# Weight casts moved from VectorE to ScalarE, and a third buffer for w_out, in a talking-heads attention and MLP kernel

## The chip, the cores and the metric

The kernel runs on one core of a Trainium2 chip. The metric is device time in microseconds (us) of one execution. The engines are TensorE (PE: matmul; PEld: its weight load), VectorE (DVE), ScalarE (ACT), GpSimd (POOL) and SyncE (SP, which here only issues DMAs).

## The reference, cut to what matters

Attention over 4 batches, 12 heads, 448 positions, head size 64, with a mix of the heads before and after the softmax; then an MLP over the 1792 tokens that come out of it:

```python
x = attn_out.transpose(0, 2, 1, 3).reshape(1792, 768)
h = x @ w_in                    # w_in  768 x 2048, float64
g = np.maximum(0.01 * h, h)
out = (g @ w_out).astype(np.float32)   # w_out 2048 x 768, float64
```

The two MLP weights come as float64 and have to become float32 on the chip.

## The kernel before, in words

**Stages.** The attention runs in 16 chunks of up to 120 query rows (4 per batch). While it runs, most of the weights are narrowed: float64 pieces of 128x384 are loaded, turned to float32 (`Narrow`, L78 to L111) and stored in a scratch tensor `w_dram`. For w_in, and for the first two blocks of w_out, this happens there. The other 14 blocks of w_out (`EARLY <= i < NF`, L321) are narrowed in the MLP itself, in its first pass.

**The MLP** has 4 passes (one for each batch, 448 tokens), each over NF = 16 blocks of 128 hidden features, so 64 blocks i. `hidden(i)` (L341) multiplies the block of w_in (part 0) with x: 18 matmuls into `psh`; ScalarE scales the result (t, L350), VectorE takes the maximum (g, L351), ScalarE casts it to float32r (gh, L352), and VectorE takes the rest (gl, L353). `project(i)` (L356) multiplies the block of w_out (part 1) with g: 18 matmuls into `pso`. Eighteen, because each float32 operand is split into a float32r value and a rest, and three of the products are made for each of 6 slices (`three`, L336).

**A weight block** comes to SBUF by `load_w(i, part)` (L319). Its tile is `wr`; part 0, and part 1 of blocks 0, 1 and from 16 on, is one DMA from `w_dram` (L325). Part 1 of blocks 2 to 15 is narrowed into `wr` in two pieces: DMA of the float64 words (craw, L90), two ScalarE copies (z, L100, and w or wr, L101), three VectorE operations (top L102, top L105, exp L108), two GpSimd operations (L109, L110), and a DMA that saves the float32 piece for later passes (L111). `prep_w(i, part)` (L328) splits the block: `wh` is the cast to float32r (L332, VectorE), `wl` the rest (L333, VectorE). All weight tags (wr, wh, wl of each part) have two buffers, from pool `w`.

**Order.** The loop at L489 writes, for i = 1 to 64: prep_w(i, 1), prep_w(i+1, 0), hidden(i), load_w(i+2, 0), load_w(i+1, 1), project(i-1), and at a pass's end the loads and splits of the next x. Dependencies and waits are put in by the framework, which also orders each engine's instructions at compile time from this program order and its own estimate of when each is ready. On the chip every engine takes its instructions in that fixed order. In the trace VectorE's order in a block of the first pass differs from the program's. Blocks 0 and 1 are loaded and block 0 and part 0 of block 1 split during the last attention chunk (L465 to L475).

The few lines that matter most:

```python
t = pl["w"].tile([P, DM], F32, tag=f"r{part}", name=f"wr{part}")   # L320
nc.vector.tensor_copy(hi, raw)                                      # L332
nc.vector.tensor_sub(lo, raw, hi.bitcast(F32))                      # L333
if i + 1 < n:                                                       # L499
    load_w(i + 1, 1)
```

Of the kernel before, what the change touches and what calls it, by code (L numbers as in the profile page):

```python
# [8 lines left out]
F32 = mybir.dt.float32  # L9
# [23 lines left out]
def kernel(  # L33
# [10 lines left out]
    nc = tc.nc  # L44
    B, P, NJ, H, D = v.shape
    S = k.shape[3]
    DM = out.shape[0]
# [248 lines left out]
    pl = {}  # L296
# [10 lines left out]
    def load_x(b, c):  # L307
        xr_t[b, c] = pl["xr"].tile([P, S], F32, tag="xr", name="xr")
        nc.sync.dma_start(xr_t[b, c], x_dram[b][:, c])

    def prep_x(b, c):
        raw = xr_t.pop((b, c))
        hi = pl["xs"].tile([P, S], F32R, tag="xh", name="xh")
        lo = pl["xs"].tile([P, S], F32R, tag="xl", name="xl")
        nc.scalar.copy(hi, raw)
        nc.vector.tensor_sub(lo, raw, hi.bitcast(F32))
        x_t[b, c] = hi, lo

    def load_w(i, part):  # L319
        t = pl["w"].tile([P, DM], F32, tag=f"r{part}", name=f"wr{part}")  # L320
        if part and EARLY <= i < NF:  # L321
            for j in range(2):
                Narrow(pl["n"], i, 2 + j, t[:, j * PIECE:(j + 1) * PIECE])()
        else:
            nc.sync.dma_start(t, w_dram[i % NF][:, part * DM:(part + 1) * DM])  # L325
        wr_t[i, part] = t

    def prep_w(i, part):  # L328
        raw = wr_t.pop((i, part))
        hi = pl["w"].tile([P, DM], F32R, tag=f"h{part}", name=f"wh{part}")  # L330
        lo = pl["w"].tile([P, DM], F32R, tag=f"l{part}", name=f"wl{part}")
        nc.vector.tensor_copy(hi, raw)  # L332
        nc.vector.tensor_sub(lo, raw, hi.bitcast(F32))  # L333
        w_t[i, part] = hi, lo

# [5 lines left out]
    def hidden(i):  # L341
        ps = pl["ps_h"].tile([P, 512], F32, tag="h", name="psh")
        for c in range(NC):
            three(ps[:, :S], w_t[i, 0], x_t[i // NF, c], c, c == 0, c == NC - 1)
        del w_t[i, 0]
        t = pl["g"].tile([P, S], F32, tag="t", name="t", bufs=1)
        g = pl["g"].tile([P, S], F32, tag="g", name="g", bufs=1)
        hi = pl["g"].tile([P, S], F32R, tag="gh", name="gh")
        lo = pl["g"].tile([P, S], F32R, tag="gl", name="gl")
        nc.scalar.activation(t, ps[:, :S], AF.Copy, scale=0.01)  # L350
        nc.vector.tensor_max(g, t, ps[:, :S])  # L351
        nc.scalar.copy(hi, g)  # L352
        nc.vector.tensor_sub(lo, g, hi.bitcast(F32))  # L353
        g_t[i] = hi, lo

    def project(i):  # L356
        b, f = divmod(i, NF)
        w, g = w_t.pop((i, 1)), g_t.pop(i)
        for c in range(NC):
            if f == 0:  # L360
                o_t[c] = pl["ps_o"].tile([P, 512], F32, tag=f"o{c}", name=f"pso{c}")
            three(o_t[c][:, :S], w, g, c, f == 0, f == NF - 1)
            if f == NF - 1:
                o = pl["o"].tile([P, S], F32, tag="o", name="o")
                (nc.scalar.copy, nc.vector.tensor_copy)[c % 2](o, o_t[c][:, :S])
                (nc.scalar, nc.sync)[c % 2].dma_start(out[c * P:(c + 1) * P, b * S:(b + 1) * S], o)
# [23 lines left out]
    for t, pat in ((kraw, ((H, ROWS), (0, H))), (kpost, ((0, H), (H, ROWS)))):  # L390

        nc.gpsimd.affine_select(
            t, t, pattern=[[-a, z] for a, z in pat], base=0, channel_multiplier=1, compare_op=ALU.is_ge, fill=0.0
        )
        nc.gpsimd.affine_select(
            t, t, pattern=[[a, z] for a, z in pat], base=H - 1, channel_multiplier=-1,
# [18 lines left out]
    for n in range(NCK):  # L415
# [4 lines left out]
        for t in range(SLOTS):  # L420
# [44 lines left out]
            if last and t == NC:  # L465
                load_w(0, 0)
                load_w(0, 1)
                load_w(1, 0)
            if last and t == NC + 2:
                prep_w(0, 0)  # L470
                prep_w(0, 1)
                load_w(1, 1)
            if last and t == NC + 4:
                prep_w(1, 0)
                load_w(2, 0)  # L475
# [10 lines left out]
    pl.update(o=pool("o", NC), n=pool("n", 2), ps_o=pool("ps_o", 1, space=PSUM))  # L486

    n = B * NF
    for i in range(1, n + 1):  # L489
        b, f = divmod(i, NF)  # L490
        if i < n:
            prep_w(i, 1)
        if i + 1 < n:
            prep_w(i + 1, 0)
        if i < n:
            hidden(i)
        if i + 2 < n:
            load_w(i + 2, 0)
        if i + 1 < n:  # L499
            load_w(i + 1, 1)  # L500
        project(i - 1)

        if b + 1 < B:
            for c in range(NC):
                if f == NF - 4 + (c > 3):
                    load_x(b + 1, c)
            if f == NF - 3:
                for c in range(4):
                    prep_x(b + 1, c)
            if f == NF - 1:  # L510
                for c in range(4, NC):
                    prep_x(b + 1, c)
# [39 lines left out]
```

## Time and profile before

| | us |
|---|---|
| median of 3 runs | 1094.42 |
| the 3 runs | 1094.42, 1084.62, 1095.0 |
| the profiled execution, device time | 1095.89 |
| its span, first to last instruction | 1094.2 |

The span is what the profile divides up; the 1.7 us between it and the device time lie around it. Busy time counts an instruction from start to end as the profiler records it, waits for a memory port included; matmuls overlap, so their durations add up to more than the time that they take. In rows of the timeline the first number is the start and the second the length in us; "x2" merges two instructions of one kind that follow each other, and a bracket gives the idle time before and what ended it.

### The profile page before, as it was taken

To read this page: it belongs to the slowest core of one execution; us is meant where nothing else is said; L and a number is where in the kernel's file an instruction comes from. 1 tells how busy PE (TensorE), PEld (TensorE's weight loads), DVE (VectorE), ACT (ScalarE), POOL (GpSimd) and SP (SyncE) were. 2 spreads that over 40 slices of the span, in tenths; PEclk is the share of its full clock that TensorE was granted. 3 is DMA by queue.
4 is the path that set the end of the run, shared out by engine and by line. 5 is a ranking of instruction groups with operands and counts; after the bars stand their busy time and mean duration, and the time that the engine had idled before them with its cause. 6 is when DMAs were issued, how large, how long until landed. Compare 5 with 4: busy or idle time off the path is not lost. (4 is left out here: it accounts for less than half of the span.)

```text
span 1094.2 us, 17821 instructions
## 1 busy us (share of the span) xinstructions
PE 1012.1 (93%) x6564; PEld 842.9 (77%) x6564; DVE 839.4 (77%) x1390; ACT 424.6 (39%) x951; POOL 444.6 (41%) x356
## 2 busy tenths in 40 slices
PE   4899889997899999999999988889999999999998
PEld 2576667775777767677768777779999999999997
DVE  6899887789888999768797599997556755565553
ACT  3664365644645646455552233332112211121111
POOL 5677764578565676546441165661000000000000
PEclk9999889998999999899999999999999999999999
DMA  5746533764354624536263455566333634353421
GB/s 184 282 161 194 190 110 119 234 198 156 119 171 158 240 70 154 177 112 216 100 230 89 136 181 177 178 179 214 102 116 103 205 102 116 104 163 101 116 89 63
DMA packets 93771, 167.11 MB, mean 153 GB/s; under 512 B 26740, under 2 KB 68724, under 8 KB 93172
## 3 DMA queue, kind: packets, MB, share of 16 engines
q1 hardware_dynamic: 91956, 163.23, 47.0%
q10 hardware_dynamic: 1728, 2.75, 0.7%
q8 instruction: 51, 0.84, 0.3%
q14 instruction: 36, 0.29, 0.1%
HBM read 103.82 MB, written 23.59 MB: 116 GB/s over the span
## 5 line engine op out<-in xcount | busy, mean ns | idle before, releaser
L211 POOL TENSOR_TENSOR rlo<-rt,rhi 120x448 fp32r<-120x448 f32 x144 | 175.3, 1221 | 141.6 <-DVE rhi L210 82.2
L332 DVE CAST wh<-wr 128x768 fp32r<-128x768 f32 x128 | 88.7, 695 | 138.3 <-PE psh L339 88.4
L256 PEld LDWEIGHTS psa<-kp,et 120*128 120x128 f32 (+2 forms) x1800 | 166.0, 174 | 35.7 <-issue 18.2
L256 PE MATMUL psa<-kp,et 120*128 120x120 f32 (+2 forms) x1800 | 179.8, 262 | 13.2 <-DVE kp L229 9.4
L216 ACT ACTIVATE et<-psm,stat 120x448 f32<-120x448 f32 x180 | 114.7, 639 | 152.7 <-DVE stat L215 151.3
L214 PE MATMUL psm<-rhi,kpre 120*120 120x448 f32 x360 | 149.5, 420 | 22.0 <-ACT et L216 21.7
L339 PE MATMUL pso<-gh,wl 128*128 128x448 f32 x384 | 141.7, 371 | 14.0 <-DVE wl L333 13.4
L339 PE MATMUL psh<-xh,wl 128*128 128x448 f32 x384 | 140.6, 366 | 3.5 <-DVE g L351 3.5
L339 PE MATMUL pso<-gl,wh 128*128 128x448 f32 x384 | 141.4, 368 | 0.0
L339 PE MATMUL pso<-gh,wh 128*128 128x448 f32 x384 | 141.4, 368 | 0.0
L339 PE MATMUL psh<-xh,wh 128*128 128x448 f32 x384 | 140.6, 366 | 0.0
L339 PE MATMUL psh<-xl,wh 128*128 128x448 f32 x384 | 140.4, 366 | 0.0
L350 ACT ACTIVATE t<-psh 128x448 f32<-128x448 f32 x64 | 34.8, 544 | 252.5 <-PE psh L339 243.2
L210 DVE CAST rhi<-rt 120x448 fp32r<-120x448 f32 x180 | 129.0, 717 | 2.3 <-DMA rt<-st 2.3
L215 DVE TENSOR_REDUCE stat<-psm 120x1 f32<-120x448 f32 x180 | 110.4, 614 | 26.4 <-PE psm L214 26.2
L333 DVE TENSOR_TENSOR wl<-wr,wh 128x768 fp32r<-128x768 f32 x128 | 123.8, 968 | 1.6
L187 ACT ACTIVATE st<-pss 120x448 f32<-120x448 f32 (+1 forms) x192 | 97.1, 551 | 57.4 <-PE pss L186 27.4
L282 PE MATMUL psx<-at,vt 128*64 128x120 f32 (+1 forms) x1152 | 109.0, 282 | 4.1 <-DVE at L264 2.7
L214 PEld LDWEIGHTS psm<-rhi,kpre 120*120 120x120 f32 x360 | 68.9, 191 | 47.0 <-ACT et L216 31.9
L282 PEld LDWEIGHTS psx<-at,vt 128*64 128x64 f32 x1152 | 68.0, 141 | 43.8 <-issue 31.5
L186 PE MATMUL pss<-kst,qlo 128*120 128x448 f32 (+1 forms) x192 | 82.3, 428 | 20.1 <-POOL kst L146 10.2
L339 PEld LDWEIGHTS pso<-gh,wl 128*128 128x128 f32 x384 | 72.9, 190 | 24.1 <-issue 14.5
(64 smaller groups left out, 1658.7 us busy)
## 6 DMA issues: line engine op xcount, KB each, us to landing
wr<-w_dram SPq DMA_DIRECT2D x114, 384.0 KB
rt<-st SPq DMA_DIRECT2D x176, 210.0 KB
craw<-in_w_moe SPq DMA_DIRECT2D x64, 384.0 KB
kraw<-in_k SPq DMA_DIRECT2D x48, 224.0 KB
qraw<-in_q SPq DMA_DIRECT2D x11, 720.0 KB
w_dram<-w SPq DMA_DIRECT2D x36, 192.0 KB
vt<-in_v SPq DMA_DIRECT2D x4, 1536.0 KB
xr<-x_dram SPq DMA_DIRECT2D x24, 224.0 KB
```

Of the source, the lines that this page charges most:

```text
L186: nc.tensor.matmul(ps[:m, :S], w[:, h, :m], k_t[b, h], start=i == 0, stop=i == 1)
L187: nc.scalar.activation(s_t[n][:m, h, :], ps[:m, :S], AF.Copy, scale=scale)
L210: nc.vector.tensor_copy(hi[:kk], raw[:kk])
L211: (nc.vector if g == 3 else nc.gpsimd).tensor_sub(lo[:kk], raw[:kk], hi[:kk].bitcast(F32))
L214: nc.tensor.matmul(ps[:kk, :S], kpre[w][:kk, :sg[g][1], :], x[:kk], start=i == 0, stop=i == 2)
L215: nc.vector.tensor_reduce(st[:kk, 0, g:g + 1], ps[:kk, :S], axis=AX.X, op=ALU.max, negate=True)
L216: nc.scalar.activation(e[:kk], ps[:kk, :S], AF.Exp, bias=st[:kk, 0, g:g + 1], accum_out=st[:kk, 1, g:g + 1])
L256: nc.tensor.matmul(ps[p0:p0 + np, w * g:w * g + nh * r], es[g][:r * H, c * P:c * P + np], kp[:r * H, g, h::step, :r], start=True, stop=True,)
L282: nc.tensor.matmul(ps[D * e:D * (e + 1), pair % 3, :m], v_t[b][up, c, h, :], at[:, c, h, :m] if c < NJ - 1 else half[up, pair, :m], start= ...
L332: nc.vector.tensor_copy(hi, raw)
L333: nc.vector.tensor_sub(lo, raw, hi.bitcast(F32))
L339: nc.tensor.matmul(ps, w[a][:, c * P:(c + 1) * P], x[e], start=first and j == 0, stop=last and j == 2)
```

## The change

`wh` is made by ScalarE's copy in place of VectorE's. Part 1 of a weight block (w_out) has three `wr` buffers in place of two and is loaded, and in blocks 2 to 15 narrowed, two blocks ahead in place of one; block 2 is loaded ahead of the loop. Part 0 keeps two buffers.

```diff
     def load_w(i, part):
-        t = pl["w"].tile([P, DM], F32, tag=f"r{part}", name=f"wr{part}")
+        t = pl["w"].tile([P, DM], F32, tag=f"r{part}", name=f"wr{part}", bufs=2 + part)
...
     def prep_w(i, part):
...
-        nc.vector.tensor_copy(hi, raw)
+        nc.scalar.copy(hi, raw)
         nc.vector.tensor_sub(lo, raw, hi.bitcast(F32))
...
     n = B * NF
+    load_w(2, 1)
     for i in range(1, n + 1):
...
         if i + 2 < n:
             load_w(i + 2, 0)
-        if i + 1 < n:
-            load_w(i + 1, 1)
+        if i + 2 < n:
+            load_w(i + 2, 1)
         project(i - 1)
```

## Rows read from the trace of the kernel before

**Rows 1.** The page: busy time by engine, and VectorE's busy tenths in 40 slices

```profile
PE 1012.1 (93%) x6564; PEld 842.9 (77%) x6564; DVE 839.4 (77%) x1390; ACT 424.6 (39%) x951; POOL 444.6 (41%) x356
...
DVE  6899887789888999768797599997556755565553
```

**Rows 2.** Windows: stretch, length, busy time by engine, TensorE's clock, DMA share, GB/s

```profile
560.00:577.00 17.00, 14.71 (x136) 10.36 (x134) 17.00 (x29) 8.87 (x22) 9.87 (x8) 0.90 0.69 225
...
616.78:745.00 128.22, 111.23 (x515) 98.16 (x516) 116.89 (x173) 45.10 (x92) 74.71 (x56) 0.97 0.60 181
...
750.00:1082.24 332.24, 332.24 (x1641) 307.87 (x1640) 192.68 (x285) 57.55 (x104) 0.00 (x0) 1.00 0.41 120
```

**Rows 3.** The chain that ended last, two pieces of the later passes

```profile
768.51 3.65 PE pso L339 x18
772.16 3.65 PE psh L339 x18
```

**Rows 4.** Waits, 592 to 745 us: total, times, longest

```profile
ACT wr L101 <- DVE wl L333: 40.0, 12, 4.8
...
PE pso L339 <- DVE wl L333: 13.4, 10, 2.7
```

**Rows 5.** Groups of instructions by line, 620 to 742 us

```profile
L109 POOL TENSOR_TENSOR wr<-wr,exp 128x384 f32<-128x384 f32 x28 | 38.2, 1373 | 86.5 <-ACT wr L101 50.8 <-DVE exp L108 25.2 <-ACT z L100 6.0
L110 POOL TENSOR_TENSOR wr<-wr,top 128x384 f32<-128x384 f32 x28 | 36.9, 1329 | 1.1
...
L332 DVE CAST wh<-wr 128x768 fp32r<-128x768 f32 x25 | 30.4, 1217 | 5.3 <-POOL wr L110 5.2
```

**Rows 6.** Timeline of VectorE, one block of the first pass

```profile
690.33 0.62 DVE L102 TENSOR_SCALAR top<-z 128x384 uint32<-128x384 uint32 x2
690.87 0.95 DVE L333 TENSOR_TENSOR wl<-wr,wh 128x768 fp32r<-128x768 f32 x1
691.74 1.01 DVE L105 SCALAR_TENSOR_TENSOR top<-z,top 128x384 uint32<-128x384 uint32 x2
692.67 0.62 DVE L108 TENSOR_SCALAR exp<-top 128x384 uint32<-128x384 uint32 x2
693.39 1.28 DVE L353 TENSOR_TENSOR gl<-g,gh 128x448 fp32r<-128x448 f32 x1
694.59 1.37 DVE L332 CAST wh<-wr 128x768 fp32r<-128x768 f32 x1
695.89 0.61 DVE L351 TENSOR_TENSOR g<-t,psh 128x448 f32<-128x448 f32 x1
696.42 1.24 DVE L333 TENSOR_TENSOR wl<-wr,wh 128x768 fp32r<-128x768 f32 x1
697.58 1.37 DVE L332 CAST wh<-wr 128x768 fp32r<-128x768 f32 x1
698.87 0.62 DVE L102 TENSOR_SCALAR top<-z 128x384 uint32<-128x384 uint32 x2
```

**Rows 7.** Timeline of GpSimd, the same block

```profile
693.17 2.38 POOL L109 TENSOR_TENSOR wr<-wr,exp 128x384 f32<-128x384 f32 x2 [3.18 <-DVE exp L108]
695.51 3.02 POOL L110 TENSOR_TENSOR wr<-wr,top 128x384 f32<-128x384 f32 x2
```

**Rows 8.** Timeline of VectorE where GpSimd is idle, end of first pass and later

```profile
743.52 1.02 DVE L332 CAST wh<-wr 128x768 fp32r<-128x768 f32 x2
744.46 0.95 DVE L333 TENSOR_TENSOR wl<-wr,wh 128x768 fp32r<-128x768 f32 x1
...
768.55 0.56 DVE L332 CAST wh<-wr 128x768 fp32r<-128x768 f32 x1 [2.10 <-PE psh L339]
```

**Rows 9.** Groups by line and shape, whole span: ScalarE's copies

```profile
L352 ACT CAST gh<-g 128x448 fp32r<-128x448 f32 x64 | 36.2, 566 | 41.3 <-DVE g L351 32.8 <-PE pso L339 8.4
...
L169 ACT CAST qhi<-qraw 128x720 fp32r<-128x720 f32 x20 | 29.2, 1513 | 0.0
...
L264 ACT COPY at<-psa 128x480 f32<-128x480 f32 x24 | 13.8, 574 | 12.2 <-PE psa L256 12.2
...
L264 ACT COPY half<-psa 128x240 f32<-128x240 f32 x24 | 8.9, 370 | 1.2 <-PE psa L256 1.1
```

## The prediction

> **What bounds the kernel now.** I read the page first. VectorE is busy 77% overall, but its 40 slices are uneven: nines at slices 24 to 27, then fives and sixes [rows 1]. So the kernel has stages with different limits, and the windows cut them. From 750 us on TensorE is busy for all of 332.24 us at full clock, while VectorE is busy for 58% and ScalarE for 17% [rows 2]. Hidden and project products follow each other there every 3.65 us [rows 3]: 7.30 us a block, which is TensorE's own pace. Nothing done on ScalarE or in buffers can shorten that part; it can only disturb it.
>
> From 616.78 to 745 us, where the 14 late blocks of w_out are narrowed, TensorE is busy for 111.23 of 128.22 us at a mean granted clock of 0.97 [rows 2]. Its loss is 17.0 us idle and some 3% of 111 us, 3.3 us, to the clock: about 20 us. This is the ceiling of what the stage can give back. The waits name who is late: project waits for wl ten times, 13.4 us in all, and ScalarE's wr copies (L101) wait for wl twelve times, 40.0 us [rows 4], because the narrowing of a block needs the buffer that an earlier wl frees.
>
> Why is wl late? VectorE's timeline of one block has no gap: from top at 690.33 to the next top at 698.87 is 8.54 us [rows 6], 1.24 us over TensorE's 7.30. But its instructions are not all at their own length. A cast takes 1.37 us here, and 1.02 us for two where GpSimd is idle [rows 6, 8]. By the spacing of starts an undisturbed cast costs VectorE (744.46 - 743.52)/2 = 0.47 us. In the stage 25 recorded casts average 1217 ns [rows 5]. The extra is time in which GpSimd works: the cast begun at 697.58 ends at 698.95, 0.42 us behind GpSimd's end at 695.51 + 3.02 = 698.53; the cast begun at 694.59 ends at 695.96, 0.41 us behind GpSimd's end at 695.55 [rows 6, 7]. And GpSimd's pairs are stretched by VectorE: 2.38 us for two with a gl (0.61 us, the length of g, which meets no stretch) between them leaves 0.88 us each, and 3.02 us with a wl (0.95) and a cast's 0.42 us inside leaves 0.83 us each. The two engines take turns.
>
> If they take turns throughout, one block costs: VectorE's casts 2 x 0.44, top 0.54, wl 2 x 0.87, L105 0.93, exp 0.54, gl 0.53 (spacings of starts, gl's taken as that of g; top's for exp, which has the same form), together 5.16; GpSimd 2 x 0.88 + 2 x 0.83 = 3.42. The sum is 8.58 us against 8.54 seen. Fourteen blocks make 120 us, most of the 128 us stretch. So it is the pair VectorE plus GpSimd, taking turns, that sets this stage; g (PSUM input) is the only operation beside GpSimd's.
>
> A page of the Trainium skill says the same more sharply. "SBUF — State Buffer", section "Who interferes with whom", calls the port pair of VectorE and GpSimd an exclusive lock, taken for a whole instruction by a copy in a two-port mode or an operation with two SBUF inputs. The 0.41 and 0.42 us tails above agree. By that rule a cast taken away gives back its 0.4 to 0.5 us; by VectorE's spacing alone (1.30 and 1.29 us a cast in rows 6) it would give back about three times as much, which is the first rival.
>
> **The change part by part.** *Casts off VectorE, late blocks.* There are 14 x 2 = 28 in the stage. What goes from the turn-taking sum is 0.41 to 0.47 us each: 11.5 to 13.2 us, I take 0.44, 12.3 us. The block goes to 8.54 - 0.88 = 7.66 us. That is still above 7.30, so TensorE keeps waiting some 0.36 us a block and the turn-taking stays the bound.
>
> *The same casts on ScalarE.* No row has a contiguous 128x768 copy. Bounds: 0.57 us (128x448) and 1.51 us (128x720, dealt with strides) [rows 9]. ScalarE's copies of 480 and 240 columns differ by 204 ns, 0.85 ns a column, so 0.566 + 320 x 0.00085 = 0.84 us, which I take. ScalarE is busy 45.10 of 128.22 us in the stage and 57.55 of 332.24 after it [rows 2]; 28 x 0.84 = 24 us more, and about 1.7 us per 7.30 us block later, fit. What they cost is delay: 0.84 against 0.47 us is 0.37 us for each cast that lies on the path. With the two blocks of lead only the casts at the stage's start and end do; two of them, 0.8 us. Bounds 0 and 28 x 0.37 = 10.4.
>
> The Trainium skill speaks against this edit: "ScalarE: Activation LUTs", section "Rules for kernel authors", gives elementwise work to VectorE as the faster engine. The lengths agree (0.84 us estimated against 0.56). Where its delay decides, the outcome is rival B; by the rows VectorE's turn is the dearer thing here.
>
> *Two blocks ahead, three buffers.* The copy of block i+1 into wr waited for wl of block i-1; now the copy of block i+2 does, in the same iteration i. The wait keeps its place in the program, but its result is due one block later, so the 40.0 us of ScalarE waits cover less that is urgent. The price is at the start: a third block may be narrowed before wl of block 2. One narrowing costs 3.42 + 0.54 + 0.93 + 0.54 = 5.4 us of turns; TensorE has spare hidden products for part of it, and the lead comes back at the end, where the last blocks run at 7.30. Bounds 0 and 5.4, I take 2.5. SP carries the same DMAs: two piece loads and two stores for a block, each block's now one iteration earlier, ahead of the next part 0 load, which can be queued behind a store that waits for GpSimd. The same bytes in 118 in place of 128 us raise the DMA share from 0.60 to 0.65; the attention's tail runs at 0.69 [rows 2], so I cost this at nothing. From 750 us on the earlier loads meet a TensorE that never waits: nothing.
>
> *Casts in the attention's tail.* From 560 to 577 us VectorE is busy for all 17.00 us and TensorE for 14.71 at a clock of 0.90 [rows 2]; three casts lie there. Bounds 0 and 2.3 us (the idle); TensorE is late by other work of VectorE too, so 0.5.
>
> Sum: 12.3 + 0.5 - 2.5 - 0.8 = 9.5 us. The profiled execution took 1095.89 us (span 1094.2 and 1.7 around it): 1086.4. It is 1.5 us above the median, so 1085.0 on the median's footing.
>
> **The rivals.**
> *A, VectorE's spacing was the bound.* Each cast gives back 1.29 us, the block would be at 5.96 us, and TensorE's 7.30 takes over. Then the loss of 20 us goes but for the start, where project and hidden need narrowing and g in turn; leaving 4 us of it gives 16 us, 1078.5. For it: no gap on VectorE. Against: the stretched lengths on both engines.
> *B, the fixed order eats it.* ScalarE takes instructions in order. The wr copies wait up to 4.8 us at its head [rows 4]; the casts now stand in that queue, and the wl behind such a cast is the one that a later copy waits for. If so every cast's 0.37 us of delay lies on the path: 12.3 + 0.5 - 2.5 - 10.4 = -0.1, no change, 1094.5. For it: those waits, and a copy-to-wl cycle that TensorE already waits for. Against: two copies (0.57 us each at most, by rows 9), cast and wl come to 0.57 x 2 + 0.84 + 0.95, under 3 us of a 7.66 us block.
> *C, slower.* In the later passes a cast waits for TensorE to free a buffer [2.10 us, rows 8], now on ScalarE, where t and gh stand. If t of block i stands behind the cast that waits for project(i-1), it is 3.65 + 0.84 us late; t, g, gh and gl, some 0.6 us each [rows 6, 9], need 2.4 us more: 6.9 of the 7.30 us that TensorE leaves. With a second cast ahead of gh it is 7.7: 0.45 us lost in each of 48 blocks, 21.6 us, on top of 1085.0: 1107. It decides from 7.30 us on. Against: VectorE has the same waits ahead of g now and TensorE loses nothing.
>
> **How the numbers follow.** Forecast 0.57, A 0.15, B 0.18, C 0.10. The forecast's own range is a gain of 5 to 14 us, 1080 to 1090. With A and B inside, and the bounds of start, delay and tail, 1073 to 1098; C and the outer end of A, under 2 in 10, are left out. A measurement tells about 1%, 10.9 us, from no change: 1083.5 and 1105.4. About half of the forecast (0.28) and A make 0.43 faster; the rest of the forecast, B and a little of C 0.49 the same; 0.08 slower.
>
> **What would show it.** Right: blocks of the first pass at about 7.7 us; no DVE casts, GpSimd's pairs shorter by the casts' turns, VectorE and GpSimd together still without a gap; ScalarE's cast 0.8 to 0.9 us; TensorE full after the first pass. A shows as a 7.30 us block with VectorE idle between; B as ScalarE's long waits with casts behind; C as TensorE waiting for gl after 750 us. I am wrong if GpSimd's operations overlap VectorE's once the casts are gone, or if the start costs more than a block's turns.

## The result, and the profile after

| | before | after |
|---|---|---|
| median of 20 runs each, same chip | 1095.11 | 1099.83 |
| ratio, 95% interval | | 1.0065 [1.0039, 1.0092] |
| the profiled execution | 1095.89 | 1096.58 |
| its span | 1094.2 | 1094.8 |
| first project matmul to the last | 616.8 to 1089.2, 472.4 | 612.5 to 1089.5, 477.0 |

The change costs 4.7 us by the medians; a gain of 9.5 was forecast, and 1099.8 lies above the range. The ratio, here and below, leaves out executions in a slower state (6 of the 20 after, one of them at 1851.84 us), so it is not the quotient of the medians; by it the change costs some 7 us. The interval excludes 1, but the change is under 2%, as are all differences in this document. The two spans differ by 0.6 us only because after's attention part, ahead of any instruction that the change touches, ran faster in its profiled execution: the first xl (L316) starts at 549.57 us before and at 544.91 after. From there to the first project it is 67.2 and 67.6 us, so the attention's tail gave nothing. In the profiled executions all of the loss lies behind the first project, and I compare that stretch, "the stage", in what follows: 4.6 us longer.

The page of the profile after, busy time by engine, and the group of the moved cast:

```profile
PE 1012.2 (92%) x6564; PEld 843.9 (77%) x6564; DVE 783.2 (72%) x1262; ACT 522.3 (48%) x1079; POOL 434.8 (40%) x356
...
L332 ACT CAST wh<-wr 128x768 fp32r<-128x768 f32 x128 | 106.2, 830 | 88.0 <-PE pso L339 82.3
```

Beside [rows 1]: 128 instructions left VectorE and went to ScalarE, 830 ns each (0.84 was estimated). VectorE is 56.2 us less busy, and the kernel is not faster. The windows after, to set beside [rows 2] (stretch, length, busy time by engine, TensorE's clock, DMA share, GB/s):

```profile
612.50:745.00 132.50, 115.88 (x514) 102.04 (x515) 114.58 (x150) 68.22 (x121) 66.70 (x56) 0.94 0.63 187
760.00:1080.00 320.00, 320.00 (x1580) 296.53 (x1579) 141.07 (x189) 121.90 (x189) 0.00 (x0) 1.00 0.38 115
```

The later passes are as they were: TensorE is busy for all of 320 us. The chain after shows the same pace as [rows 3]; its last lines:

```profile
1075.30 3.65 PE pso L339 x18
1078.95 3.65 PE psh L339 x18
1082.60 7.31 PE pso L339 x36
```

So the loss is in the first pass. A matmul at full pace takes 0.2027 us, the 3.65 us of the chain (3.648 before rounding) by 18. Over the 133 us from the first project matmul, before ran 539 of them, 109.3 us' worth: 23.7 us lost. After ran 516: 28.4 us lost.

The waits after, 592 to 745 us (engine and line that waited, what for, total, times, longest), to set beside [rows 4]:

```profile
ACT z L100 <- DVE top L105: 18.6, 17, 2.5
...
PEld pso L339 <- DVE gl L353: 9.0, 6, 2.1
...
ACT wr L101 <- DVE wl L333: 6.9, 7, 1.8
PE pso L339 <- DVE gl L353: 6.8, 6, 1.8
...
PE pso L339 <- DVE wl L333: 4.8, 2, 2.9
```

The long wait of the wr copies for wl went, as the change means it to: 40.0 us became 6.9. But project now waits for gl as well as for wl: six waits, 9.0 us of them at the weight loads and 6.8 at the matmuls, where the whole view that [rows 4] is from has no wait of TensorE for gl. Its matmuls' waits for wl fell from 13.4 to 4.8 us. Why gl is late stands in VectorE's timeline after, from one g to the next, which is one block of TensorE's work (start, length, instruction):

```profile
681.32 0.62 DVE L351 TENSOR_TENSOR g<-t,psh 128x448 f32<-128x448 f32 x1
681.86 0.87 DVE L102 TENSOR_SCALAR top<-z 128x384 uint32<-128x384 uint32 x1
682.65 1.76 DVE L333 TENSOR_TENSOR wl<-wr,wh 128x768 fp32r<-128x768 f32 x1
684.33 0.55 DVE L105 SCALAR_TENSOR_TENSOR top<-z,top 128x384 uint32<-128x384 uint32 x1
684.80 0.61 DVE L353 TENSOR_TENSOR gl<-g,gh 128x448 fp32r<-128x448 f32 x1
685.34 0.35 DVE L102 TENSOR_SCALAR top<-z 128x384 uint32<-128x384 uint32 x1
685.61 0.35 DVE L108 TENSOR_SCALAR exp<-top 128x384 uint32<-128x384 uint32 x1
685.87 0.55 DVE L105 SCALAR_TENSOR_TENSOR top<-z,top 128x384 uint32<-128x384 uint32 x1
686.34 1.76 DVE L333 TENSOR_TENSOR wl<-wr,wh 128x768 fp32r<-128x768 f32 x1
688.03 1.17 DVE L108 TENSOR_SCALAR exp<-top 128x384 uint32<-128x384 uint32 x1
689.12 0.35 DVE L102 TENSOR_SCALAR top<-z 128x384 uint32<-128x384 uint32 x1
689.50 1.25 DVE L105 SCALAR_TENSOR_TENSOR top<-z,top 128x384 uint32<-128x384 uint32 x1
690.79 1.05 DVE L108 TENSOR_SCALAR exp<-top 128x384 uint32<-128x384 uint32 x1
691.77 0.61 DVE L351 TENSOR_TENSOR g<-t,psh 128x448 f32<-128x448 f32 x1
```

Count the narrowing: L102, L105 and L108 stand there three times each, so three pieces of w_out pass in one block, where [rows 6] shows two. Again there is no gap. The block takes 10.45 us in place of 8.54; the five from block 7 to block 12 take 9.94 on the mean (project 7 starts at 664.33, project 12 at 714.01; before, 674.66 and 717.56, 8.58 on the mean). It was not so from the start: 60 us behind the first project the two kernels had lost about the same, 12.6 us after and 13.0 before. VectorE used the turns that the casts left free to narrow further ahead, and TensorE paid for it. GpSimd's last narrowing instruction and the project that starts then, in the timeline after:

```profile
714.04 1.59 POOL L110 TENSOR_TENSOR wr<-wr,top 128x384 f32<-128x384 f32 x1
```
```profile
714.01 0.47 PE L339 MATMUL pso<-gh,wl 128*128 128x448 f32 x1 [0.95 <-ACT gh L352]
```

That project is the 13th (block 12): narrowing is over and three blocks of it lie ahead unused. The same two places in the timeline of the kernel before:

```profile
740.40 1.61 POOL L110 TENSOR_TENSOR wr<-wr,top 128x384 f32<-128x384 f32 x1
```
```profile
743.75 0.44 PE L339 MATMUL pso<-gh,wl 128*128 128x448 f32 x1 [0.45 <-DVE wl L333]
```

There it is the 16th (block 15): narrowing ended just in time, with nothing ahead. The narrowing itself ends 103.1 us behind the first project after, 125.2 before.

**The theory.** Call it N. Until the last narrowing ends, VectorE and GpSimd take turns with hardly a gap, and every piece that is narrowed early takes turns that the wl and gl of the current block needed. By the terms of the prediction, with T from the first project to the end of narrowing and n the blocks that TensorE has done in it (36 matmuls each):

T = 4 + 14 x 5.4 + n x 2.27 (two wl at 0.87, a gl at 0.53), and n x 0.88 more where VectorE casts.

The 4 us are fitted, the same for all kernels; the traces have a measure for them, the time within T in which VectorE and GpSimd are both idle: 4.0 us before, 4.1 after, 4.0 to 4.1 in e2, e3, e8 and e12 below, 5.3 in e1. TensorE loses T - 7.3 n; that much is bookkeeping, and what can fail is the formula for T. From there on TensorE runs near its full pace (in the rest of the 133 us before loses another 0.7 us, after 2.1), so hardly anything done ahead is paid back. With the casts on ScalarE the loss is 79.6 - 5.03 n: by the formula each block not done when narrowing ends costs 5 us. The rivals that the runs below had to tell apart: B of the prediction (the cast is late in ScalarE's queue), L (the third buffer and the lead alone), and K (TensorE's clock: of the 28.4 us lost after, 16.6 are idle and 11.8 are matmuls over their full pace, at a granted clock of 0.94; before it was 17.0 and 6.8 at 0.97).

### The profile page after: what moved, and what is told of

Read it like the earlier page. It is cut to its first block, busy times and chain, and to the rows that moved or that the text cites. A ratio compares the mean times of both kernels' runs of the same rounds, so it can differ in the third digit from the quotient of the medians.

```text
span 1094.8 us, 17877 instructions
## 1 busy us (share of the span) xinstructions
PE 1012.2 (92%) x6564; PEld 843.9 (77%) x6564; DVE 783.2 (72%) x1262; ACT 522.3 (48%) x1079; POOL 434.8 (40%) x356
## 4 chain that ended last, share of the span: by engine, by line
PE 60%; DVE 24%; DMA 6%; issue 4%; ACT 2%; POOL 1%; SPq 1%; ACTq 0%; DVEq 0%; POOLq 0%
PE psh L339 18%; PE pso L339 17%; PE psa L256 8%; PE psx L282 7%; PE psm L214 6%; PE pss L186 4%; DVE rhi L210 4%; DVE top L105 3%; DMA craw<-in_w_moe 3%; DVE stat L215 2%; DVE kst L145 2%; DVE top L102 2%; DVE wl L333 2%; DMA rt<-st 2%; DVE at L264 1%
## 5 line engine op out<-in xcount | busy, mean ns | idle before, releaser
L333 DVE TENSOR_TENSOR wl<-wr,wh 128x768 fp32r<-128x768 f32 x128 | 129.9, 1015 | 87.8 <-ACT wh L332 82.9
L256 PE MATMUL psa<-kp,et 120*128 120x120 f32 (+2 forms) x1800 | 179.1, 261 | 13.9 <-DVE kp L229 10.7
L339 PE MATMUL pso<-gl,wh 128*128 128x448 f32 x384 | 144.6, 377 | 6.8 <-DVE gl L353 6.8
L332 ACT CAST wh<-wr 128x768 fp32r<-128x768 f32 x128 | 106.2, 830 | 88.0 <-PE pso L339 82.3
L339 PE MATMUL pso<-gh,wh 128*128 128x448 f32 x384 | 144.1, 375 | 0.0
L215 DVE TENSOR_REDUCE stat<-psm 120x1 f32<-120x448 f32 x180 | 110.4, 613 | 23.7 <-PE psm L214 23.7
L351 DVE TENSOR_TENSOR g<-t,psh 128x448 f32<-128x448 f32 x64 | 39.6, 619 | 122.3 <-ACT t L350 122.3
```

Source lines behind the costliest of these rows:

```text
L215: nc.vector.tensor_reduce(st[:kk, 0, g:g + 1], ps[:kk, :S], axis=AX.X, op=ALU.max, negate=True)
L256: nc.tensor.matmul(ps[p0:p0 + np, w * g:w * g + nh * r], es[g][:r * H, c * P:c * P + np], kp[:r * H, g, h::step, :r], start=True, stop=True,)
L339: nc.tensor.matmul(ps, w[a][:, c * P:(c + 1) * P], x[e], start=first and j == 0, stop=last and j == 2)
```

## The experiments

All ratios are to the kernel before, run on the same chip in the same batch. Here are all of them beforehand. T and n as above; "turns" is T by the formula; loss is 133 us from the first project less its matmuls at 0.2027, split in idle and over pace; wl is how many wl VectorE executes before its last narrowing instruction. The expectations of e1 to e4 call an earlier form of N "theory T"; that is not the T of this table.

```
                                T  turns   n    wl | loss = idle + over pace | stage  ratio
before                        125.2 123.7 14.0  33 | 23.7   17.0    6.8      | 472.4
after                         103.1 103.4 10.5  27 | 28.4   16.6   11.8      | 477.0  1.0065
e1 cast only                  107.7 105.9 11.6  29 | 22.7   17.0    5.7      | 471.3  0.9988
e2 ahead only                 122.6 121.2 13.2  32 | 27.4   18.0    9.4      | 482.7  1.0070
e3 cast, third buffer         103.0 103.4 10.5  27 | 26.8   19.7    7.1      | 475.4  1.0016
e4 narrowing on VectorE       117.2   -   13.9   - | 15.8   11.5    4.4      | 464.5  0.9909
e5 cast, narrowing on VectorE 110.5   -   13.9   - |  8.7    5.9    2.8      | 457.5  0.9855
e6 change, narrowing on Vect. 114.4   -   14.2   - | 11.2    6.4    4.8      | 459.7  0.9905
e7 cast, narrowing held       129.0 112.5 14.5  35 | 24.4   18.2    6.1      | 473.0  0.9990
e8 change, three ahead        103.2 103.7 10.6  27 | 25.6   15.7    9.9      | 474.2  1.0009
e9 cast, second piece held    122.5 111.8 14.2  35 | 18.9   12.6    6.2      | 467.6  0.9914
e12 cast, first piece held    109.2 108.2 12.6  31 | 17.5   11.0    6.4      | 466.1  0.9928
```

### The two halves of the change: e1, e2, e3

e1, the cast alone:

```diff
-        nc.vector.tensor_copy(hi, raw)
+        nc.scalar.copy(hi, raw)
```

> Only the casts move to ScalarE; w_out has two buffers and one block of lead as before. Theory T (VectorE and GpSimd take turns, and the second block of lead costs turns that TensorE then waits for): the 28 casts' turns are given back, so 8 to 12 us faster than before, the stretch from the first project matmul to the last matmul 461 to 465 us in place of 472.8, blocks of the first pass about 7.7 us apart. Rival S (the casts in ScalarE's queue are the harm): slower than before by 3 to 8 us, as the changed kernel is.

Measured: 1090.74 us, ratio 0.9988 [0.9950, 1.0027], stage 471.3. A miss for what I held then: no change where 8 to 12 us were expected. Nor is it slower by 3 to 8 us, as the rival there had it. The waits of e1, 592 to 745 us:

```profile
ACT wr L101 <- DVE wl L333: 19.9, 10, 3.6
```

Half of the wait that held the narrowing back is gone (40.0 in [rows 4]) without a third buffer, and narrowing ends 17.5 us earlier, at n = 11.6. The casts did give back their turns: with them on VectorE the formula asks for 116.1 us at this n, and T is 107.7. But the turns went into a lead.

e2, the lead alone (the change with the cast back on VectorE):

```diff
-        nc.scalar.copy(hi, raw)
+        nc.vector.tensor_copy(hi, raw)
```

> Only the third buffer and the second block of lead; the casts stay on VectorE. Theory T: two more narrowings of 5.4 us are done before TensorE needs them, and nothing pays for them, so 10 to 18 us slower than before, the stretch from the first project to the end 482 to 491 us. Rival S: no change within 3 us, or a little faster.

Measured: 1098.99 us, ratio 1.0070 [1.0035, 1.0105]: slower, as the whole change is. Its stage of 482.7 us falls into the expected span by accident. The chain of e2:

```profile
775.48 3.72 PE pso L339 x18
779.20 3.72 PE psh L339 x18
```

Its later passes ran at 3.72 us per 18 matmuls, at a granted clock of 1.00, where all others show 3.65 at 1.00. Over the 1739 matmuls behind the end of narrowing that is 1739 x 0.07 / 18 = 6.8 us, and without it the stage is 475.9, 3.5 over before. So the sign was right and the size too large: the lead alone costs 3.5 us by the stage and 7.7 by the ratio, not 10 to 18. How many of e2's other runs had the slower pace, and so how much of the ratio is the lead's, no trace shows. By the time alone, rival L would do for the whole loss of the change (1.0070 against 1.0065); what it does not say is why the casts, alone, gain nothing.

e3, e1 with the third buffer but one block ahead:

```diff
-        t = pl["w"].tile([P, DM], F32, tag=f"r{part}", name=f"wr{part}")
+        t = pl["w"].tile([P, DM], F32, tag=f"r{part}", name=f"wr{part}", bufs=2 + part)
```

> Casts on ScalarE and the third buffer, but w_out is loaded one block ahead as before. Theory T: the lead costs, not the buffer, so within 3 us of the kernel with the casts alone. Rival L (the third buffer lets the fixed order run ahead by itself): near the changed kernel, 3 to 8 us slower than before.

Measured: 1093.11 us, ratio 1.0016 [0.9978, 1.0054]. The intervals of e1 and e3 overlap, so by time they are not told apart; by the profile e3's stage is 4.1 us longer, with T, n and wl those of the whole change. My expectation, within 3 us of e1, is missed by the stage; the time is at its edge (2.4 us by the medians, 3.1 by the ratios). VectorE's order tells more: from its first wl to its last narrowing instruction, 170 instructions, it is the same in e3 as in the changed kernel, name by name. With three buffers the compiled order runs as far ahead as it does with the load written two blocks ahead, and writing the load earlier adds nothing.

e3 also speaks on K. It has after's order, T and n, and another split of the loss: 19.7 idle and 7.1 over pace, against 16.6 and 11.8. The windows of after, then of e3, from the first project to the end of narrowing (columns as above):

```profile
612.53:715.64 103.11, 87.05 (x379) 75.44 (x379) 96.48 (x124) 54.27 (x98) 66.70 (x56) 0.93 0.64 187
```
```profile
610.21:713.24 103.03, 83.88 (x379) 72.41 (x379) 96.50 (x124) 54.28 (x98) 66.70 (x56) 0.97 0.66 187
```

At a granted clock of 0.93 and of 0.97 TensorE does the same 379 matmuls in the same time. While the turns bind, a lower clock only moves loss from idle time to matmuls over their pace. Behind the narrowing it does add. The windows there of after, then of e8, the run with a fourth buffer:

```profile
715.64:745.53 29.89, 29.36 (x137) 27.09 (x138) 18.29 (x27) 13.95 (x24) 0.00 (x0) 0.94 0.63 189
```
```profile
711.33:741.08 29.75, 29.75 (x149) 27.57 (x148) 18.31 (x27) 14.97 (x26) 0.00 (x0) 1.00 0.70 215
```

After loses 29.89 - 137 x 0.2027 = 2.1 us there: from 716.4 to 719.8 us its granted clock is 0.50, the level of 1.2 GHz, and its matmuls start 0.37 us apart. e8 loses nothing. So of the 4.7 us that after's profile loses more than before's (28.4 against 23.7), 3.2 lie in the narrowing and 1.4 behind it, where that clock stands. The ratios of after (1.0065) and e3 (1.0016) have overlapping intervals.

### GpSimd out of the turns: e4, e5, e6

If turn-taking is the cause, the late narrowing is better off with no GpSimd in it. e4 is the kernel before with:

```diff
-            nc.gpsimd.tensor_mul(w, w, exp.bitcast(F32))
-            nc.gpsimd.tensor_add(w, w, top.bitcast(F32))
+            eng = nc.gpsimd if self.w is None else nc.vector
+            eng.tensor_mul(w, w, exp.bitcast(F32))
+            eng.tensor_add(w, w, top.bitcast(F32))
```

e5 is the same with the cast on ScalarE, e6 the whole change with it.

> The kernel before, but the product and sum of the narrowing in the MLP's first pass run on VectorE in place of GpSimd, so no two engines take turns there. Theory T: 3.42 us of GpSimd's turns for a block become 4 VectorE operations of about 0.47 us, 1.9 us; 8.54 - 3.42 + 1.88 = 7.0 us is under TensorE's 7.30, so 10 to 18 us faster than before and casts back at 0.56 us. Rival V (VectorE's own work is the bound and GpSimd relieves it): four more operations a block, 14 x 1.9 = 26 us slower.

> Casts on ScalarE with two buffers and one block of lead, and the narrowing's product and sum on VectorE instead of GpSimd. Theory N (while narrowing runs, VectorE and GpSimd take turns without a gap; each late block costs a fixed sum of turns, and what TensorE loses is that sum less the blocks that it gets done meanwhile): a narrowing costs 3.9 us of VectorE in place of 5.4 us of turns, and a block of the MLP 2.8 us, 6.7 together, under TensorE's 7.30; only the start's waits stay. First project to last project matmul 454 to 459 us (before 472.4, casts alone 471.3), 13 to 18 us faster than before. Rival S (casts in ScalarE's queue cost what they save): no better than the narrowing on VectorE with the casts left there (464.5 us, 10 us faster).

> The changed kernel (casts on ScalarE, three buffers, two blocks ahead) with the narrowing's product and sum on VectorE. Theory N: with no turns to take, VectorE has 0.6 us a block to spare, so the lead costs little: within 4 us of the same kernel with one block of lead, 10 to 17 us faster than before. Rival L2 (the third buffer and the lead cost time by themselves, turns or not): 4.6 us and more behind the kernel with one block of lead.

Measured: e4 1083.24 us, 0.9909 [0.9869, 0.9949]; e5 1076.37 us, 0.9855 [0.9805, 0.9904]; e6 1082.72 us, 0.9905 [0.9867, 0.9943]. All three are faster than both kernels, and e5 is the best of the study; its stage is within the 454 to 459 us that N expected. e4's gain, 10 us by the ratio and 7.9 by the stage, is at or under the lower end of the 10 to 18 us expected. e6 is a miss: it was to come within 4 us of e5, and its median is 6.35 us behind, on the side of rival L2 (4.6 us and more), though its stage is only 2.2 behind. With n no lower than e5's (14.2 and 13.9), N has no term for that, so by the time the lead has a cost here that N does not explain. The groups of VectorE in e5, 612 to 712 us (count | busy, mean ns):

```profile
L110 DVE TENSOR_TENSOR wr<-wr,exp 128x384 f32<-128x384 f32 x27 | 14.9, 552 | 0.0
L111 DVE TENSOR_TENSOR wr<-wr,top 128x384 f32<-128x384 f32 x26 | 14.4, 552 | 0.0
L105 DVE SCALAR_TENSOR_TENSOR top<-z,top 128x384 uint32<-128x384 uint32 x26 | 14.3, 552 | 0.0
```

The two operations take 552 ns on VectorE, spaced 0.47 us; on GpSimd they held the turn for 0.83 to 0.88 us each. The engine that has more to do does its work sooner. The windows of e5 (columns as above):

```profile
640.00:660.00 20.00, 20.00 (x101) 18.53 (x100) 18.27 (x39) 11.51 (x21) 0.00 (x0) 1.00 0.69 223
660.00:680.00 20.00, 20.00 (x100) 18.54 (x99) 17.73 (x37) 12.41 (x23) 0.00 (x0) 1.00 0.73 212
680.00:700.00 20.00, 20.00 (x100) 18.53 (x99) 19.80 (x42) 13.13 (x24) 0.00 (x0) 1.00 0.78 243
```

TensorE is full from 640 to 700 us, in the middle of the narrowing. And here the casts do pay: e5's stage is 7.0 us shorter than e4's, a little over half of the 12.3 us that the prediction's first step gave them (the intervals of the two ratios overlap). n is 13.9 in both, so here the move of the casts did not shift narrowing forward either.

### The same instructions in another order: e12, e9, e7

N says that e1 needs nothing but its turns in another order. In e12 VectorE's work on the first piece of a block is held behind the wl of part 0 (an order at compile time, no new wait on the chip between engines):

```diff
+            with tc.issue_after(wls[-1]) if j in (0,) else ExitStack():
                 Narrow(pl["n"], i, 2 + j, t[:, j * PIECE:(j + 1) * PIECE])()
...
-        nc.vector.tensor_copy(hi, raw)
-        nc.vector.tensor_sub(lo, raw, hi.bitcast(F32))
+        nc.scalar.copy(hi, raw)
+        ins = nc.vector.tensor_sub(lo, raw, hi.bitcast(F32))
+        if part in (0,):
+            wls.append(ins.ins)
```

> Casts on ScalarE, two buffers, one block of lead, and only the first piece of a narrowing held, behind wl of part 0 of the block now in work. Compiled, 31 wl stand ahead of the last narrowing. Theory N: about one block more than with the casts alone (29 wl, 471.3 us) is done during the narrowing, worth about 5 us: first project to last 464 to 468 us, 4 to 8 us faster than before. Rival (the order of VectorE is not what decides): within 2 us of 471.

Measured: 1086.46 us, ratio 0.9928 [0.9884, 0.9971], stage 466.1, as N expected: 5.2 us under e1 with the same instructions. (The intervals of the two ratios overlap a little; that the order does it rests on the stage and on the ratio's fall by 0.6%.) VectorE's timeline of e12, from g to g:

```profile
660.37 0.61 DVE L356 TENSOR_TENSOR g<-t,psh 128x448 f32<-128x448 f32 x1
660.90 1.52 DVE L336 TENSOR_TENSOR wl<-wr,wh 128x768 fp32r<-128x768 f32 x1
662.35 1.43 DVE L102 TENSOR_SCALAR top<-z 128x384 uint32<-128x384 uint32 x2
663.70 0.54 DVE L105 SCALAR_TENSOR_TENSOR top<-z,top 128x384 uint32<-128x384 uint32 x1
664.16 0.61 DVE L358 TENSOR_TENSOR gl<-g,gh 128x448 fp32r<-128x448 f32 x1
664.70 0.54 DVE L105 SCALAR_TENSOR_TENSOR top<-z,top 128x384 uint32<-128x384 uint32 x1
665.17 0.62 DVE L108 TENSOR_SCALAR exp<-top 128x384 uint32<-128x384 uint32 x2
665.70 0.95 DVE L336 TENSOR_TENSOR wl<-wr,wh 128x768 fp32r<-128x768 f32 x1
667.69 0.62 DVE L356 TENSOR_TENSOR g<-t,psh 128x448 f32<-128x448 f32 x1 [1.04 <-ACT t L355]
```

Two pieces to a block, and this one takes 7.32 us, near the 7.66 that the prediction gave such a block and TensorE's 7.30. VectorE even has a gap of 1.04 us. The next block takes 8.81 us with gaps of 0.90 and 1.92: at places the chain through the other engines, not the turns, is now what VectorE waits for. Over the whole stretch n rose from 11.6 to 12.6, and the loss fell from 22.7 to 17.5 us, 5.2 us for about one block; N has 5.03.

e9 holds the second piece behind the part 1 wl in the same way (`j in (1,)`, `if part:`), e7 both pieces (`with tc.issue_after(last_wl[0]): load_w(i + 1, 1)`).

> Casts on ScalarE, two buffers, one block of lead, and only the second piece of a block's narrowing held, on VectorE, behind wl of the block before. Compiled, 35 of the 128 wl stand ahead of the last narrowing in VectorE's order (before 33, casts alone 29, the change 27). Theory N: with as many blocks done during the narrowing as before, and no casts to take turns, the loss falls: 448.5 us of matmuls and 7 to 13 us lost, first project to last 456 to 462 us, 8 to 14 us faster than before. If a chain of waits replaces the turns, as when both pieces were held (473.0), it stays above 468.

> Casts on ScalarE, two buffers, one block of lead, and an order that holds the VectorE work of the narrowing of block i+1 behind wl of block i; GpSimd keeps its part. Theory N: the casts' turns were lost because the narrowing used them to run ahead; held back, they go to wl and gl, and the gain of the casts appears: first project to last 460 to 466 us (casts alone 471.3), 5 to 11 us faster than before. Against it stands a chain (narrow, GpSimd, cast, wl) of about 7.2 us a block, which may take its place and leave the time near 471. Rival S: no change from the casts alone.

Measured: e9 1085.41 us, 0.9914 [0.9878, 0.9950], stage 467.6, above the 456 to 462 of N alone, though its time is within the 8 to 14 us faster that N expected; e7 1094.49 us, 0.9990 [0.9962, 1.0018], stage 473.0, a miss: 5 to 11 us faster were expected, with a chain named that might prevent it. In both T is above the turns, by 10.7 and 16.5 us. Two windows and two waits (592 to 745 us) of e7 say why:

```profile
640.00:660.00 20.00, 18.03 (x81) 16.13 (x80) 13.09 (x26) 10.38 (x18) 8.57 (x8) 0.91 0.59 195
660.00:680.00 20.00, 17.26 (x79) 15.54 (x78) 12.61 (x23) 10.62 (x20) 10.84 (x10) 0.92 0.52 162
```
```profile
DVE wl L335 <- ACT wh L334: 30.4, 16, 3.6
...
PEld psh L343 <- DVE g L355: 17.5, 7, 3.7
```

VectorE is busy for 13 of 20 us and no longer the bound. Held so late, the narrowing of a block, its cast and its wl follow one another in a chain, and VectorE waits at the head of its order for wh while hidden waits for g. In e9 the same wait of wl for wh comes to 25.5 us. Too little lead costs too: e7 has n = 14.5 and still loses 24.4 us.

### More lead: e8

e8 is the change with four buffers and the load three blocks ahead (`bufs=2 + 2 * part`, `load_w(3, 1)` ahead of the loop, `load_w(i + 3, 1)` in it).

> The change with one step more: four buffers and three blocks of lead. Theory N: another narrowing is done before TensorE needs it; a block of lead at the end costs about 5 us, so 2 to 6 us slower than the changed kernel, first project to last 479 to 483 us, unless the fixed order does not use the fourth buffer. Rival (the lead costs only at the start, once): no slower than the changed kernel.

Measured: 1094.73 us, ratio 1.0009 [0.9974, 1.0044], stage 474.2. 2 to 6 us more than the change were expected, unless the fixed order left the fourth buffer unused, and so it did: T, n and wl are those of the change, and VectorE's order differs from after's only in its last dozen instructions. So e8 tells little of a longer lead. Its ratio lies under that of the change (the intervals overlap slightly); by the profiles the 2.8 us between the stages are mostly the 2.1 us that after loses behind the narrowing and e8 does not.

## Why the prediction was wrong, point by point

**The step that failed** is the first of the sum: "What goes from the turn-taking sum is 0.41 to 0.47 us each ... I take 0.44, 12.3 us. The block goes to 8.54 - 0.88 = 7.66 us." The turns did come free: the terms give T within 2 us for after, e1, e2, e3, e8 and e12. But the step took for granted that a block of TensorE and one narrowing stay paired, so that a free turn goes to what TensorE waits for. VectorE has a fixed order, and that order put three pieces, in the block shown, where two had been. At n = 14 as before, the loss would have gone from 79.6 - 4.15 x 14 = 21.5 to 79.6 - 5.03 x 14 = 9.2 us, which is the 12.3 us of the step; at the 10.5 that it came to, it is 26.8. Of the 3.5 blocks between, 2.4 go with the casts alone (e1, n = 11.6): 2.4 x 5.03 = 12.1 us, all of the step's gain. Where the order is partly put right by hand (e12) about one of those 2.4 blocks is back, with 5.2 us, and where GpSimd is out of the turns the same casts give 7.0 us (e4 to e5).

**The lead** was the second error, of size and of reason. "The price is at the start ... the lead comes back at the end, where the last blocks run at 7.30. Bounds 0 and 5.4, I take 2.5." It does not come back: 7.30 is also the pace of every block behind the narrowing, so a lead there is worth nothing, and every block narrowed early costs its turns while they are scarce. The third buffer takes n from 11.6 (e1) to 10.5 (e3, after), by the formula 1.1 x 5.03 = 5.5 us; the stages give 4.1 and 5.7, at the outer bound. After has a lead of three blocks when narrowing ends, before none. The sign "the start costs more than a block's turns" did stand among what would make the forecast wrong, but the price was not paid at the start, where the losses are alike for 60 us; it was paid in the second half of the narrowing.

**The wait that I read as a loss looks like a brake.** The 40.0 us of ScalarE's wr copies [rows 4] would, by N, have kept the narrowing from running ahead with VectorE's and GpSimd's turns, and so have given wl its place. e1 halved the wait and gained nothing; the change took nearly all of it and lost. No run changes the wait alone with the order kept, so this is argued, not shown.

**What held:** the turn-taking and its terms; the cast's 0.83 us; the later passes, full as before, so rival C (1107 us) did not come; the attention's tail, within its bounds at 0. Rival A falls: with n = 11.6 and two casts a block, e1 took 23 casts off the stretch, T came out 8.4 us below the formula with them, 0.36 us a cast, not 1.29. Rival B's 1094.5 us is near e1's time, but not by its mechanism: the wr copies' waits for wl became shorter, not longer, and from the first project to the end of narrowing no wl of e1, e3 or after waits for ScalarE's wh. The loss that came was in none of the rivals. The one on the slower side looked at ScalarE's queue in the later passes, where there was slack, and not at VectorE's order in the first pass, where there was none.

**What stays open.** Why the compiled order moves narrowing forward when the casts leave is argued from wl falling from 33 to 29 and 27, not shown: the estimates by which it is made are not in the trace. That the order decides rests on e12 (another order, another loss) and e3 (the same order, the same T and n); why e6 is slower than e5 is open. Stages come from one profiled execution each; differences of a few us between them rest on the ratios as well, and where a ratio's interval includes 1 (e1, e3, e7, e8) the stage alone says little of the time.

## What to carry to other kernels

Where two engines share turns without a gap, an instruction that leaves frees turns, and the fixed order decides who gets them: look for what else in that order is ready, and count whether it is wanted in this stage or only later. Work ahead has a price while the resource is scarce, and it pays back only if there is slack later that it can fill; a buffer wait off the critical path may be the brake that keeps such work from running ahead, so ask of each long wait what would be done in its place. Before work is moved off the busy engine, try moving the other engine's out of the turns: the two operations held the turn for 0.83 to 0.88 us on GpSimd and 0.47 on VectorE, and giving the busier engine more to do was worth more than the change meant to relieve it.

## What the runs showed of the hardware that I had not expected

TensorE's full pace is not one number. The later passes of e2 ran all at 3.72 us per 18 matmuls, 1.9% slower than in any other profile here, both at a granted clock of 1.00. Over a stage that is 6.8 us, more than the 4.7 us of the change, so before two profiles are compared their pace is to be read in a stretch where TensorE never waits. What sets the pace no run here shows.
